# Reading the moving operand backwards in both layers of a convolution and squared-ReLU kernel

## The chip, the cores and the metric

The kernel runs on one core of a Trainium2 chip. The metric is the time of one execution on the device in microseconds; less is better. The profile is one more execution, taken by the hardware profiler, with every instruction's start and duration.

## The reference

The input is x, 8 sequences of 4096 tokens with 192 features. Each feature is convolved over the last 7 tokens of its sequence with softmax weights that belong to its head (8 heads of 24 features). The result goes, token by token, through a two-layer network with 2048 hidden units whose activation is a squared ReLU:

```python
w = np.exp(weight - weight.max(-1, keepdims=True))
w = w / (w.sum(-1, keepdims=True) + 1e-09)
out = np.einsum('hk,bskhg->bshg', w, x_unf)      # x_unf: the last 7 tokens, zeros before the first
x = out.reshape(B * S, D)                        # 32768 x 192
h = x @ w_in                                     # 192 x 2048
r = np.maximum(h, 0.0)
g = s * (r * r) + b
return (g @ w_out).astype(np.float32)            # 2048 x 192
```

The inputs are fp32 except the weights of the network, which come in as float64 words and are converted in the kernel.

## The kernel before

Data lies transposed: features on the 128 partitions, tokens along a partition. The 32768 tokens are 32 super-blocks n of 1024, each two blocks j of 512 tokens. The hidden units are NPAIR = 8 pairs p of two chunks of 128. One step (n, j, p) takes 512 tokens through one pair.

To keep fp32 accuracy at the speed of the type fp32r, which carries fewer mantissa bits, every operand is split into a high and a low part, both fp32r, and a product is three matmuls: weights high by data low, weights high by data high, weights low by data high.

Layer one is the function first. The 192 features are three chunks of 64; the tiles sA, wA, tB and wB hold the convolved tokens, high and low, in such an arrangement that one half of the partitions (rows 0 to 63) works on one chunk of 128 hidden units and the other half (rows 64 to 127) on the other. Each inner call both (line 531) issues two matmuls, one for each half of the rows, with weights of 64 x 128 and a moving operand of 64 x 512. A call of first is 18 matmuls, and fills the PSUM tile h, 128 x 2 x 512: hidden units on partitions, tokens along them, one bank for each chunk.

Between the layers ScalarE takes the ReLU of h into q (line 545) and squares it in place (line 552), VectorE rounds it to the high part qh (line 554) and subtracts to get the low part ql (line 559). All four are elementwise.

Layer two is the function second. Its inner both (line 614) again issues two matmuls, for the two halves of the rows of qh or ql, which are summed into two different PSUM accumulators: w_outB gives the output features 128 to 191 (for the high and the low part of the weights side by side), w_outA the features 0 to 127. A call is 20 matmuls. The accumulators run over all 8 pairs of a block, and are then added, scaled with s and stored. Super-block 0, in which the weights are still being converted, uses second_whole instead, with full-height matmuls of 128 x 128 weights (lines 576, 577, 581 to 583), 10 a step. The very last step of the kernel has its own function last (lines 673, 674 and 686), also with 10 full-height matmuls.

The order of the work on TensorE, VectorE and ScalarE is written out by hand: the calls are traced in the order in which they are to run. Finished steps wait in a Python list, queue, and layer two is issued LAG = 2 steps behind layer one; at the first pair of a block it is held back one step longer, after which two steps of layer two follow each other. While this goes on, VectorE computes the convolution of the super-block to come (lines 161 and 163), and the tiles are swapped and stored by DMAs of the SyncE queue. In the head, before any of this is under way, TensorE computes part of the first convolution in plain fp32 with diagonal matrices as weights (line 257, function conv_tensor): tap k reads 512 columns that begin k columns into xA or xB. The function split_tensor (line 230) and the sums for the bias (function biases) use TensorE as well. None of these three is touched by the change.

Of the kernel before, what the change touches and what calls it, by code (L numbers as in the profile page):

```python
# [17 lines left out]
P = 128  # L18
# [19 lines left out]
def conv_attention_then_squared_relu_mlp(  # L38
# [23 lines left out]
    nc = tc.nc  # L62
# [5 lines left out]
    NF = 2 * NPAIR  # L68
# [206 lines left out]
    def w_in(part, p, chunk, rows):  # L275
        return W[rows, p, part, chunk * P : (chunk + 1) * P]

    def w_outA(part, f, rows=slice(0, P)):
        return W[rows, f // 2, part, CI + f % 2 * P :][:, 0:P]

    def w_outB(f, rows=slice(0, P)):
        return WB[rows, f // 2, f % 2, :]
# [239 lines left out]
    def first(n, j, p, meanwhile=None):  # L522
        h = ps_h.tile([P, 2, BLK], F32, name="h")
        halves = [tok[n].half(j, i) for i in range(2)]

        def both(w, part, at, start, stop):

            for i in range(2):
                chunk = halves[i][at]
                rows = slice(i * HB, (i + 1) * HB)  # L530
                nc.tensor.matmul(  # L531
                    h[:, i, :], w_in(w, p, chunk[0], rows), chunk[part], start=start, stop=stop
                )

        for at in (0, 2, 1):
            both(0, 1, at, at == 0, False)
            both(0, 2, at, False, False)
            both(1, 1, at, False, at == 1)
            if meanwhile and at == 0:
                meanwhile()  # L540
        return h
# [22 lines left out]
    def accumulators(n, j, p):  # L564
        if p == 0:
            acc[n, j] = [ps_o.tile([P, BLK], F32, name=f"acc{k}") for k in (1, 2, 1, 2)[: 4 if n else 2]]
        return acc[n, j]

    def second_whole(n, j, p, qh, ql):


        a1, a2 = accumulators(n, j, p)
        for i in range(2):
            f = 2 * p + i
            st, sp = f == 0, f == NF - 1
            nc.tensor.matmul(a2, w_outB(f), qh[:, i, :], start=st, stop=False)  # L576
            nc.tensor.matmul(a2, w_outB(f), ql[:, i, :], start=False, stop=sp)  # L577
        for i in range(2):
            f = 2 * p + i
            st, sp = f == 0, f == NF - 1  # L580
            nc.tensor.matmul(a1, w_outA(1, f), qh[:, i, :], start=st, stop=False)  # L581
            nc.tensor.matmul(a1, w_outA(0, f), qh[:, i, :], start=False, stop=False)  # L582
            nc.tensor.matmul(a1, w_outA(0, f), ql[:, i, :], start=False, stop=sp)  # L583
        if p == NPAIR - 1:
            t0 = n * SUP + j * BLK
            oA = outs.tile([P, BLK], F32, name="oA")
            nc.scalar.activation(oA, a1, AF.Identity, scale=sb)
            oC = outs.tile([DB, BLK], F32, name="oC", bufs=1)
            nc.scalar.activation(oC, a2[DB:P, :], AF.Identity, scale=sb[DB:P])  # L589
            oB = outs.tile([P, BLK], F32, name="oB")[0:DB]  # L590
            nc.vector.scalar_tensor_tensor(
                oB, a2[0:DB, :], sb[0:DB], oC, op0=ALU.mult, op1=ALU.add
            )
            unbiased.append((oA, outT[0:P, t0 : t0 + BLK], 0))
            unbiased.append((oB, outT[P:D, t0 : t0 + BLK], 2))
            del acc[n, j]
# [7 lines left out]
    def second(n, j, p, qh, ql):  # L604
        if (n, j, p) == steps[-1]:
            return last(n, j, qh, ql)
        accs = accumulators(n, j, p)

        ends = [NF - 1, NF - 1 if (n, j) != steps[-1][:2] else NF - 3]

        def both(to, w, f, q, start=False, stop=False):
            for i in range(2):
                r = slice(i * HB, (i + 1) * HB)
                nc.tensor.matmul(  # L614
                    accs[to + 2 * i], w(f, r), q[r, f % 2, :],
                    start=start and f == 0, stop=stop and f == ends[i],
                )

        for f in (2 * p, 2 * p + 1):
            both(1, w_outB, f, qh, start=True)  # L620
            both(1, w_outB, f, ql, stop=True)
        for f in (2 * p, 2 * p + 1):
            both(0, loA, f, qh, start=True)
            both(0, hiA, f, qh)
            both(0, hiA, f, ql, stop=True)
        if p == NPAIR - 1:
            t0 = n * SUP + j * BLK
            early = (n, j) == (1, 0)

            o = {}  # L630
            for k, name in ((1, "oB"), (0, "oA")):
                o[k] = outs.tile([P, BLK], F32, name=name)
                o[k + 2] = outs.tile([P, BLK], F32, name=name + "2", bufs=1)
                nc.scalar.activation(
                    o[k], accs[k], AF.Identity, scale=sb, bias=0.0 if early else bias[:, k : k + 1]
                )
                nc.scalar.activation(o[k + 2], accs[k + 2], AF.Identity, scale=sb)  # L637
            nc.gpsimd.tensor_tensor(o[1], o[1], o[3], op=ALU.add)  # L638

            oC = outs.tile([DB, BLK], F32, name="oC", bufs=1)  # L640
            nc.sync.dma_start(oC, o[1][DB:P])
            nc.gpsimd.tensor_tensor(o[0], o[0], o[2], op=ALU.add)
            toA, toB = outT[0:P, t0 : t0 + BLK], outT[P:D, t0 : t0 + BLK]
            oB = o[1][0:DB] if early else oC
            if not early:
                nc.sync.dma_start(toA, o[0])
            nc.gpsimd.tensor_tensor(oB, oC, o[1][0:DB], op=ALU.add)
            if early:
                unbiased.extend(((o[0], toA, 0), (oB, toB, 2)))
            else:  # L650
                nc.sync.dma_start(toB, oB)
            del acc[n, j]

    def upper_sums(accs):

        uA = outs.tile([P, BLK], F32, name="oA2", bufs=1)
        uB = outs.tile([DB, BLK], F32, name="oC", bufs=1)
        nc.scalar.activation(
            uB, accs[3][DB:P], AF.Identity, scale=sb[DB:P], bias=bias[DB:P, 1:2]
        )  # L660
        nc.scalar.activation(uA, accs[2], AF.Identity, scale=sb, bias=bias[:, 0:1])
        nc.vector.scalar_tensor_tensor(
            uB, accs[3][0:DB], sb[0:DB], uB, op0=ALU.mult, op1=ALU.add
        )
        return uA, uB

    def last(n, j, qh, ql):

        accs = accumulators(n, j, NPAIR - 1)
        uA, uB = upper_sums(accs)  # L670
        t0 = n * SUP + j * BLK
        for f in (NF - 2, NF - 1):
            nc.tensor.matmul(accs[1], w_outB(f), qh[:, f % 2, :], start=False, stop=False)
            nc.tensor.matmul(accs[1], w_outB(f), ql[:, f % 2, :], start=False, stop=f == NF - 1)
        oB = outs.tile([P, BLK], F32, name="oB")[0:DB]
        nc.vector.scalar_tensor_tensor(
            oB, accs[1][0:DB], sb[0:DB], uB, op0=ALU.mult, op1=ALU.add
        )
        nc.vector.scalar_tensor_tensor(
            oB, accs[1][DB:P], sb[DB:P], oB, op0=ALU.mult, op1=ALU.add  # L680
        )
        nc.sync.dma_start(outT[P:D, t0 : t0 + BLK], oB)
        oA = outs.tile([P, BLK], F32, name="oA")
        for f in (NF - 2, NF - 1):
            for w, q in ((loA, qh), (hiA, qh), (hiA, ql)):
                nc.tensor.matmul(
                    accs[0], w(f, slice(0, P)), q[:, f % 2, :],
                    start=False, stop=f == NF - 1 and q is ql,
                )
        for k, e in enumerate((nc.scalar, nc.sync)):  # L690
            c = slice(k * BLK // 2, (k + 1) * BLK // 2)
            nc.vector.scalar_tensor_tensor(
                oA[:, c], accs[0][:, c], sb, uA[:, c], op0=ALU.mult, op1=ALU.add
            )
            e.dma_start(outT[0:P, t0 + c.start : t0 + c.stop], oA[:, c])
# [65 lines left out]
    with in_order(nc.vector, nc.scalar, nc.tensor):  # L761
        with in_order(nc.sync):
            head()
        headed = last_of(nc.sync)
        for p in range(NPAIR):
            if p > 1:
                if p + 3 < NPAIR:
                    with headed():
                        fetch(p + 3)
                pair(p)  # L770
            if p > 0 and p not in TWICE:
                while len(queue) > (LAG if p < NPAIR - 1 else 0):
                    second_whole(*queue.pop(0))
# [3 lines left out]
    for n, j, p in steps:  # L777
# [7 lines left out]
        with begun() if n == 1 else ExitStack():  # L785
            h = first(n, j, p)
# [62 lines left out]
```

## Time and profile before

| | us |
|---|---|
| median of 3 runs | 2234.78 (2234.44 to 2234.82) |
| span of the profiled execution, first to last instruction | 2232.9 |
| TensorE matmuls busy | 2226.4 |
| TensorE weight loads busy | 1829.1 |
| VectorE busy | 1753.5 |
| ScalarE busy | 1286.4 |
| GpSimd busy | 317.8 |

The span leaves out what lies ahead of the first and behind the last instruction, so it is a little under the time of a run. In the rows, PE is TensorE's matmuls, PEld its weight loads, DVE is VectorE, ACT ScalarE, POOL GpSimd and SP SyncE. A row of groups gives line, engine, operation, output and inputs, their sizes, the count, the busy time in us and the mean duration in ns, and behind the second bar the idle time of the engine just before them with what ended it. Matmuls overlap, so their durations do not add up to time: what counts is the distance from one start to the next. PEclk is the clock that TensorE was granted, in tenths of full speed. A row of the chain or of the timeline begins with the start and the duration in us. A row of waits has the engine and what waited, the releaser, the time in total, the number and the longest.

### The profile page before, as it was taken

The page shows a single profiled execution, that of the slowest core. Times are in us where ns is not written, and L with a number is a line of the kernel's source. Part 1 is how long each engine was busy: PE and PEld are TensorE (multiplying, and loading weights), DVE is VectorE, ACT ScalarE, POOL GpSimd, SP SyncE. Part 2 cuts the span into 40 slices and gives each one's busy share as a digit, 9 for nine tenths or more (in the row PEclk, how much of TensorE's full clock was granted, in tenths as well). Part 3 has the DMA queues.
Part 4 walks back from the last instruction along what each step waited for, and adds up shares of the span by engine and source line. Part 5 has one row for each costly group of instructions (what it writes and reads, how often), then busy time and mean ns, then how long its engine had stood idle before and what let it go on. Part 6 is the DMA issues. An engine that isn't in the chain of part 4 may idle for free.

```text
span 2232.9 us, 45081 instructions
## 1 busy us (share of the span) xinstructions
PE 2226.4 (100%) x19330; PEld 1829.1 (82%) x19330; DVE 1753.5 (79%) x1995; ACT 1286.4 (58%) x1410; POOL 317.8 (14%) x205
## 2 busy tenths in 40 slices
PE   9999999999999999999999999999999999999999
PEld 6788888888888888888888888888888888888887
DVE  8898778777787787777877878778777787787764
ACT  8755555655555555555555555555655555556554
POOL 0022101111011011110110111111101111011110
PEclk9999999999999999999999999999999999999999
DMA  5113112121121111211111111112121121111110
GB/s 180 34 43 87 40 46 62 48 58 44 44 58 53 53 44 45 56 53 53 43 51 50 53 53 53 48 43 62 51 55 44 44 58 53 53 44 42 46 39 17
DMA packets 46168, 117.51 MB, mean 53 GB/s; under 512 B 7760, under 2 KB 8016, under 8 KB 45968
## 3 DMA queue, kind: packets, MB, share of 16 engines
q1 hardware_dynamic: 45824, 114.50, 18.6%
q8 instruction: 151, 2.47, 0.5%
q14 instruction: 49, 0.40, 0.1%
q10 hardware_dynamic: 144, 0.13, 0.0%
HBM read 31.64 MB, written 25.17 MB: 25 GB/s over the span
## 4 chain that ended last, share of the span: by engine, by line
PE 98%; DVE 1%; ACT 1%; DMA 0%; issue 0%; SPq 0%; DVEq 0%
PE acc L614 50%; PE h L531 46%; DVE accA L163 0%; PE acc L576 0%; ACT q L552 0%; DVE ql L559 0%; PE acc L577 0%; PE acc L583 0%; PE acc L582 0%; PE acc L581 0%; ACT qh L554 0%; ACT q L545 0%; DMA xA<-in_xA 0%; DVE t L315 0%; ACT oC L589 0%
## 5 line engine op out<-in xcount | busy, mean ns | idle before, releaser
L545 ACT ACTIVATE q<-h 128x1024 f32<-128x1024 f32 x512 | 525.5, 1026 | 902.8 <-PE h L531 900.4
L559 DVE TENSOR_TENSOR ql<-q,qh 128x1024 fp32r<-128x1024 f32 x512 | 656.7, 1283 | 56.3 <-ACT qh L554 2.6
L554 DVE CAST qh<-q 128x1024 fp32r<-128x1024 f32 x497 | 370.1, 745 | 395.7 <-ACT q L552 393.3
L614 PE MATMUL acc<-qh,W 64*128 64x512 f32 x3960 | 609.9, 386 | 0.0
L552 ACT ACTIVATE q<-q 128x1024 f32<-128x1024 f32 x512 | 543.6, 1062 | 15.9
L614 PEld LDWEIGHTS acc<-qh,W 64*128 64x128 f32 x3960 | 370.9, 184 | 77.9
L531 PE MATMUL h<-sA,W 64*128 64x512 f32 x3072 | 432.4, 387 | 0.0
L531 PE MATMUL h<-wA,W 64*128 64x512 f32 x3072 | 431.6, 386 | 0.0
L531 PE MATMUL h<-tB,W 64*128 64x512 f32 x1536 | 429.9, 386 | 0.0
L531 PE MATMUL h<-wB,W 64*128 64x512 f32 x1536 | 429.9, 386 | 0.0
L614 PE MATMUL acc<-ql,WB 64*128 64x512 f32 x1980 | 385.7, 386 | 0.4 <-DVE ql L559 0.4
L614 PE MATMUL acc<-qh,WB 64*128 64x512 f32 x1980 | 385.6, 386 | 0.0
L614 PE MATMUL acc<-ql,W 64*128 64x512 f32 x1980 | 385.5, 386 | 0.0
L638 POOL TENSOR_TENSOR oB<-oB,oB 128x512 f32<-128x512 f32 x61 | 115.2, 1889 | 1672.7 <-ACT oB L637 1672.7
L163 DVE SCALAR_TENSOR_TENSOR accA<-xA,tap,accA 128x512 f32<-128x512 f32 x378 | 341.5, 903 | 6.8
L531 PEld LDWEIGHTS h<-sA,W 64*128 64x128 f32 x3072 | 287.3, 184 | 62.9 <-issue 1.1
L531 PEld LDWEIGHTS h<-wA,W 64*128 64x128 f32 x3072 | 287.8, 184 | 60.4
L531 PEld LDWEIGHTS h<-tB,W 64*128 64x128 f32 x1536 | 282.6, 184 | 40.5 <-issue 0.2
L531 PEld LDWEIGHTS h<-wB,W 64*128 64x128 f32 x1536 | 282.5, 184 | 20.1
L614 PEld LDWEIGHTS acc<-ql,WB 64*128 64x128 f32 x1980 | 185.5, 184 | 40.1 <-DVE ql L559 1.3
L614 PEld LDWEIGHTS acc<-ql,W 64*128 64x128 f32 x1980 | 185.5, 184 | 39.0
L614 PEld LDWEIGHTS acc<-qh,WB 64*128 64x128 f32 x1980 | 185.5, 184 | 38.8
(115 smaller groups left out, 1035.4 us busy)
## 6 DMA issues: line engine op xcount, KB each, us to landing
wA<-sA SPq DMA_DIRECT2D x126, 256.0 KB, 3.6
outT<-oA SPq DMA_DIRECT2D x63, 256.0 KB, 2.0
wB<-tB SPq DMA_DIRECT2D x60, 256.0 KB, 3.4
xA<-in_xA SPq DMA_DIRECT2D x24, 515.0 KB, 3.6
xB<-in_xB SPq DMA_DIRECT2D x32, 259.0 KB, 2.6
oC<-oB SPq DMA_DIRECT2D x61, 128.0 KB, 2.2
outT<-oC SPq DMA_DIRECT2D x60, 128.0 KB, 2.3
words<-in_w SPq DMA_DIRECT2D x7, 768.0 KB, 6.2
```

The source lines that it names most:

```text
L163: nc.vector.scalar_tensor_tensor(acc, src, w[:, k : k + 1], acc, op0=ALU.mult, op1=ALU.add)
L531: nc.tensor.matmul(h[:, i, :], w_in(w, p, chunk[0], rows), chunk[part], start=start, stop=stop)
L545: nc.scalar.activation(q, h, AF.Relu)
L552: nc.scalar.activation(q, q, AF.Square)
L554: cast(qh, q)
L559: nc.vector.tensor_tensor(ql, q, qh.bitcast(F32), op=ALU.subtract)
L614: nc.tensor.matmul(accs[to + 2 * i], w(f, r), q[r, f % 2, :], start=start and f == 0, stop=stop and f == ends[i],)
L638: nc.gpsimd.tensor_tensor(o[1], o[1], o[3], op=ALU.add)
```

## The change

Every matmul of the two layers reads its moving operand from the last column to the first: the slice of 512 columns gets a step of minus one. The operand's tile, size and type, the weights and the output are as before. Layer one so writes the tokens of a block into h in reverse, the elementwise steps keep them in that order in q, qh and ql, and layer two, which reads qh and ql from the last column to the first, writes them into its accumulators in their own order. The matmuls of the head's convolution, of split_tensor and of the bias read upwards as before. The instructions of each engine, their order and their waits are the same in both programs.

```diff
@@ first @@
-                    h[:, i, :], w_in(w, p, chunk[0], rows), chunk[part], start=start, stop=stop
+                    h[:, i, :], w_in(w, p, chunk[0], rows), chunk[part][:, ::-1], start=start, stop=stop
@@ second_whole @@
-            nc.tensor.matmul(a2, w_outB(f), qh[:, i, :], start=st, stop=False)
-            nc.tensor.matmul(a2, w_outB(f), ql[:, i, :], start=False, stop=sp)
+            nc.tensor.matmul(a2, w_outB(f), qh[:, i, ::-1], start=st, stop=False)
+            nc.tensor.matmul(a2, w_outB(f), ql[:, i, ::-1], start=False, stop=sp)
...
-            nc.tensor.matmul(a1, w_outA(1, f), qh[:, i, :], start=st, stop=False)
-            nc.tensor.matmul(a1, w_outA(0, f), qh[:, i, :], start=False, stop=False)
-            nc.tensor.matmul(a1, w_outA(0, f), ql[:, i, :], start=False, stop=sp)
+            nc.tensor.matmul(a1, w_outA(1, f), qh[:, i, ::-1], start=st, stop=False)
+            nc.tensor.matmul(a1, w_outA(0, f), qh[:, i, ::-1], start=False, stop=False)
+            nc.tensor.matmul(a1, w_outA(0, f), ql[:, i, ::-1], start=False, stop=sp)
@@ second @@
-                    accs[to + 2 * i], w(f, r), q[r, f % 2, :],
+                    accs[to + 2 * i], w(f, r), q[r, f % 2, ::-1],
@@ last @@
-            nc.tensor.matmul(accs[1], w_outB(f), qh[:, f % 2, :], start=False, stop=False)
-            nc.tensor.matmul(accs[1], w_outB(f), ql[:, f % 2, :], start=False, stop=f == NF - 1)
+            nc.tensor.matmul(accs[1], w_outB(f), qh[:, f % 2, ::-1], start=False, stop=False)
+            nc.tensor.matmul(accs[1], w_outB(f), ql[:, f % 2, ::-1], start=False, stop=f == NF - 1)
...
-                    accs[0], w(f, slice(0, P)), q[:, f % 2, :],
+                    accs[0], w(f, slice(0, P)), q[:, f % 2, ::-1],
```

## The prediction

> **What bounds the kernel now.** I read the page's first parts before anything else, since they say whether there is any engine whose work decides the end.
>
> ```profile
> PE 2226.4 (100%) x19330; PEld 1829.1 (82%) x19330; DVE 1753.5 (79%) x1995; ACT 1286.4 (58%) x1410; POOL 317.8 (14%) x205
> PEclk9999999999999999999999999999999999999999
> PE 98%; DVE 1%; ACT 1%; DMA 0%; issue 0%; SPq 0%; DVEq 0%
> PE acc L614 50%; PE h L531 46%; DVE accA L163 0%; PE acc L576 0%; ACT q L552 0%; DVE ql L559 0%; PE acc L577 0%; PE acc L583 0%; PE acc L582 0%; PE acc L581 0%; ACT qh L554 0%; ACT q L545 0%; DMA xA<-in_xA 0%; DVE t L315 0%; ACT oC L589 0%
> ```
>
> TensorE is busy for the whole span, its granted clock never falls, and the chain of work that ended last is 98% TensorE: 50% of it is layer two (line 614), 46% layer one (line 531). A busy TensorE can still be one that waits inside the pipeline, so I next read what it waited for, in the list of waits for that engine alone.
>
> ```profile
> PE acc L388 <- POOL xA L145: 1.0, 1, 1.0
> PE acc L230 <- ACT sA L227: 0.4, 1, 0.4
> PE acc L614 <- DVE ql L559: 0.4, 1, 0.4
> PE acc L230 <- ACT hiB L227: 0.2, 1, 0.2
> ```
>
> That is the whole list: 2.0 us in four waits, three of them in the head. After the head, one wait of 0.4 us is on record. So nothing that another engine does sets the pace; the pace is the rate at which TensorE takes matmuls. The chain in order of time gives this rate. It has one piece of 40 layer-two matmuls in each block of 512 tokens (two of the drained steps back to back), and I quote the first and the last of a run of such pieces that are all the same distance apart.
>
> ```profile
> 203.55 4.53 PE acc L614 x40
> 1822.85 4.53 PE acc L614 x40
> ```
>
> Between these two starts lie 1619.30 us, and 47 blocks at 34.453 us each. A block is 8 steps p, and a step is 18 matmuls of layer one and 20 of layer two. These are issued in twos, one on rows 0 to 63 and one on rows 64 to 127 of the array, which run side by side; I call such a pair a slot. 19 slots a step and 8 steps a block make 152 slots, so a slot takes 34.453 / 152 = 226.66 ns. The timeline of one step in the middle shows the same thing in single instructions.
>
> ```profile
> 1000.34 0.84 PE L531 MATMUL h<-sA,W 64*128 64x512 f32 x6
> 1001.02 0.39 PE L531 MATMUL h<-tB,W 64*128 64x512 f32 x1
> 1001.70 0.84 PE L531 MATMUL h<-wA,W 64*128 64x512 f32 x6
> ```
>
> From the sA reads to the first tB read there are 3 slots in 0.68 us, and again 3 from there to the wA reads: 227 ns each, within the rounding of the rows. A single matmul is shown as 386 ns long, but since it overlaps its neighbours, the distance from start to start is what counts. That the distance holds to a hundredth over 47 blocks, whatever VectorE, ScalarE and the DMAs do beside it, tells me that it belongs to the instruction itself.
>
> The number of slots comes from the groups of instructions by line.
>
> ```profile
> L614 PE MATMUL acc<-qh,W 64*128 64x512 f32 x3960 | 609.9, 386 | 0.0
> L531 PE MATMUL h<-sA,W 64*128 64x512 f32 x3072 | 432.4, 387 | 0.0
> L531 PE MATMUL h<-wA,W 64*128 64x512 f32 x3072 | 431.6, 386 | 0.0
> L531 PE MATMUL h<-tB,W 64*128 64x512 f32 x1536 | 429.9, 386 | 0.0
> L531 PE MATMUL h<-wB,W 64*128 64x512 f32 x1536 | 429.9, 386 | 0.0
> L614 PE MATMUL acc<-ql,WB 64*128 64x512 f32 x1980 | 385.7, 386 | 0.4 <-DVE ql L559 0.4
> L614 PE MATMUL acc<-qh,WB 64*128 64x512 f32 x1980 | 385.6, 386 | 0.0
> L614 PE MATMUL acc<-ql,W 64*128 64x512 f32 x1980 | 385.5, 386 | 0.0
> L576 PE MATMUL acc<-qh,WB 128*128 128x512 f32 x32 | 13.0, 407 | 0.0
> ```
>
> Layer one has 3072 + 3072 + 1536 + 1536 = 9216 matmuls of 64 rows, 4608 slots. Layer two has 3960 + 3 x 1980 = 9900, 4950 slots. The first two blocks use full-height matmuls instead, five groups of 32 like the last row, 160 slots of one matmul each, and the function last has 10 more. Together 9728 slots, and 9728 x 226.66 ns = 2204.9 us of the 2232.9 us span. The 28.0 us that are left are the head up to the first layer-one matmul, its gaps, and the tail. The runs' median of 2234.78 us is 1.9 us above the span; I carry these 1.9 us through unchanged.
>
> **The change part by part.** All of it is one thing: the start and the sign of the step of the moving operand in the matmuls of lines 531, 576, 577, 581 to 583, 614, 673, 674 and 686. The operand's pattern starts at its last column and steps by minus one; its size, its type, its partitions, the weights and the PSUM output, which is written from first to last column as before, stay. Layer one therefore leaves h in reversed token order, the squaring on ScalarE and VectorE is elementwise and carries the order along, and layer two reverses it back into acc, so that what is stored is in order.
>
> Instructions: none is added or removed on any engine, and the order and the waits of each engine's list are those of before. So there is no queue that a step is moved past, no DMA more or less, and no new wait: 0 us, with one answer. The data that each matmul needs are the same tiles, and each tile is waited for as a whole before its first column is read, so that reading the last column first starts nothing earlier or later: 0 us. ScalarE, VectorE and GpSimd read and write the same addresses in the same direction: 0 us.
>
> What is left is the price of a descending read in TensorE, once for each of the 9728 slots. Of it the trace of before has no instance: every operand in it ascends, so this price has to be bounded by rows. The nearest rows on where a read begins are those of the convolution in the head, which TensorE does in plain fp32 at line 257. Tap k reads 512 columns that begin k columns into the tile, so its reads begin at every place in a short stretch of memory, and each tap is two records on the timeline.
>
> ```profile
> 7.57 3.17 PE L257 MATMUL acc<-xB,q 128*128 128x512 f32 x7
> 10.57 1.88 PE L257 MATMUL acc<-xA,q 128*128 128x512 f32 x4
> 12.96 4.46 PE L257 MATMUL acc<-xA,q 128*128 128x512 f32 x10
> 17.34 0.98 PE L531 MATMUL h<-sA,W 64*128 64x512 f32 x6
> ```
>
> The first stretch is 7 records (the later taps, xB) in 10.57 - 7.57 = 3.00 us up to the next start, 428.6 ns each. The second is 4 records (taps 0 and 1): less the last record's own 592 ns, (1.88 - 0.59) / 3 = 430 ns. The third is 10 records (taps 2 to 6): (4.46 - 0.59) / 9 = 430 ns. They agree within 1.4 ns although they begin at different offsets. So a start at another column than the tile's first costs between nothing and 1.4 ns here, at a rate that is about half that of the kernel's main matmuls. Per slot that is 0 to 1.4 ns, over 9728 slots 0 to 13.6 us. I take 0, because most of these 1.4 ns is the rounding of the rows.
>
> For the rate of the descending read itself the far bound is the same rows read another way: the slowest steady pass over 512 columns that TensorE shows with its clock fully granted takes 428.6 ns against 226.66 ns. If a descending fp32r read fell to that rate, a slot would cost 201.9 ns more and the kernel 9728 x 0.2019 = 1964 us more. The other end is below nothing: the same pass halved, as if fp32r streamed exactly twice as fast as a plain pass, is 214.3 ns, so that 12.4 ns of each slot are not explained by the streaming of columns; if the direction removed all of them, the kernel would lose 9728 x 0.0124 = 120.6 us. Between these ends I take 0: with the step's size unchanged, a descending read touches the same words in the same number of steps, and the nearest row for it is the ascending read at 226.66 ns.
>
> To these 12.4 ns a rule of the Trainium skill can be held. Its page "TensorE: Matmul & The Clock Gate", section "Back-to-back issue gap", gives N / 2.4 + 2.5 ns from one warm matmul to the next, 215.8 ns for 512 columns, which would make 9728 slots an estimated 2099 us; the trace disagrees with 226.66 ns and 2205 us, and the measurement decides. The page does not say what fills the difference.
>
> Another page of the Trainium skill, "Advanced Engine Details and Errata", section "SBUF Cachelines", says that reads run at full rate as long as successive ones fall into the same line of 16 bytes, two in a line at the least. By that rule a step of minus one fp32 word, with four reads in each line, would leave the sum as it is; no run here shows it so far.
>
> The sum: 2232.9 + 0 = 2232.9 us of span, and with the 1.9 us around it 2234.8 us.
>
> **The rivals.** The first is slower by little: a price at each start. The place is the beginning of each matmul's read, at the end of a tile instead of its first column. Since TensorE has no idle time to hide it, it adds up 9728 times. It decides from 0.2% on, that is 4.47 us, or 0.46 ns per slot. At the 1.4 ns of the tap rows it makes 2234.8 + 13.6 = 2248.4 us. For it speaks that nothing covers even half a nanosecond; against it that taps with seven different starts show no pitch that grows.
>
> The second is slower by much: the descending read is not streamed at full rate. The same instructions, but every column pays. At the pitch of the plain fp32 passes the result is 2234.8 + 1964 = 4199 us, and anything between is possible. For it speaks that no descending operand exists in this trace and that no other matmul in it takes columns as fast as these, so that a fetch which joins neighbouring words only upwards would be felt at once. Against it: the slot's 226.66 ns is the same for 64 and 128 rows and over all sources, so the read shows no sign of being near a limit that varies. VectorE could not become late in its place: a slower TensorE gives the others more time.
>
> The third is faster: the unexplained 12.4 ns go. If they were a cost at the turn from one matmul's last address back to the next one's first, the direction could matter. All of it gone would give 2234.8 - 120.6 = 2114 us. TensorE would still be the bound, since VectorE has room:
>
> ```profile
> 600.00:1000.00 400.00, 400.00 (x3532) 330.58 (x3532) 314.23 (x347) 227.11 (x245) 59.79 (x38) 1.00 0.19 51
> ```
>
> In 400 us of the middle, VectorE is busy for 314.23 us (third figure) and ScalarE for 227.11 us, and a gain of 12.4 ns in 226.66 would shorten these 400 us to 378. Against this rival speaks that a matmul which turns from one operand to the next jumps in either direction, and both directions jump equally far.
>
> **How the numbers follow.** The forecast, no price, gets 0.77. The small price at a start gets 0.09, the rate that falls 0.09, the gain 0.05. That the edit changes nothing on the chip because the pattern would be undone on the way is within the first case, as its time is the same. A measurement of this kernel can tell 0.2%, about 4.5 us, from no change; so within 0.2% is 0.77, slower 0.18, faster 0.05. The predicted time is 2234.8 us. The range begins 0.2% below it, at 2230.3, and reaches up to the small price's 2248.4; it holds 0.77 + 0.09 and leaves out 0.14, the large loss and the gain.
>
> **What would show it.** If the forecast is right, the same pieces of 40 matmuls in the chain stand 34.45 us apart, a matmul of lines 531 and 614 is 386 ns long, and the list of TensorE's waits stays at four short ones. A price at the start would show as blocks of up to 152 x 1.4 = 213 ns more, with matmuls that are hardly longer. A read that falls in rate would show in the duration of each matmul and in a block of up to 65 us, with VectorE's and ScalarE's idle time growing by as much and their own durations as before. A gain would show as blocks down to 32.6 us. If the span moved while a block stayed at 34.45 us, the head or the tail would be the place, and my reasoning about the waits would be wrong.

## The result and the profile after

The changed kernel takes 2297.49 us (median of 4 runs, 2297.40 to 2297.74) against 2234.80 us of the kernel before on the same chip (4 runs): a ratio of 1.0281, with a 95% interval of 1.0268 to 1.0293. It is 62.7 us slower. The forecast was no change, and the time lies outside the range given.

The first parts of the page after show which engine has the loss.

```profile
PE 2290.3 (100%) x19330; PEld 1839.0 (80%) x19330; DVE 1752.8 (76%) x1995; ACT 1287.3 (56%) x1410; POOL 316.8 (14%) x205
PEclk9999999999999999999999999999999999999999
PE 100%; DVE 0%; DVEq 0%; issue 0%; POOL 0%; POOLq 0%
L614 PE MATMUL acc<-qh,W 64*128 64x512 f32 x3960 | 624.4, 394 | 0.0
L531 PE MATMUL h<-sA,W 64*128 64x512 f32 x3072 | 443.0, 394 | 0.0
L559 DVE TENSOR_TENSOR ql<-q,qh 128x1024 fp32r<-128x1024 f32 x512 | 658.2, 1285 | 56.9 <-ACT qh L554 3.3
```

The counts are those of before, the granted clock is full, and VectorE's and ScalarE's operations are as long as they were (ql: 1285 ns against 1283). Only TensorE's matmuls have grown, from 386 to 394 ns, in both layers alike. The list of what TensorE waited for has become shorter, one row of 1.0 us in the head. So no wait has come in. The chain in order of time has its pieces of 40 layer-two matmuls again:

```profile
206.94 4.67 PE acc L614 x40
...
1164.53 4.67 PE acc L614 x40
```

Between these two lie 27 blocks, 957.59 / 27 = 35.466 us each; before it was 34.453. With 152 slots in a block (a slot is a pair of matmuls on the two halves of the rows, started side by side), a slot now takes 233.33 ns, 6.67 ns more than the 226.66 of before. In the timeline of the changed kernel every three slots lie 0.70 us apart, where there were 0.68:

```profile
1000.57 0.86 PE L531 MATMUL h<-sA,W 64*128 64x512 f32 x6
1001.27 0.39 PE L531 MATMUL h<-tB,W 64*128 64x512 f32 x1
1001.97 0.86 PE L531 MATMUL h<-wA,W 64*128 64x512 f32 x6
```

9728 slots x 6.67 ns = 64.9 us, and the span has grown by 2295.8 - 2232.9 = 62.9 us. The 2 us between belong to the first 121 us. The 25th step of layer one starts at 121.3 us before and at 122.3 us after, only 1.0 us later; from there on each slot pays in full. Up to there, 1.0 us of TensorE's waits has gone from the list, and in super-block 0 not every slot of before was as short as 226.7 ns: its full-height matmuls started 228.4 ns apart in the mean (149 distances, six gaps of more than 300 ns left out), where they now start 233.4 apart. Behind the head the loss is thus one steady price at each slot. What is left to find is what the price is for.

### The profile page after: what moved, and what is told of

It reads as the page before. It is cut to its first block, busy times and chain, and to the rows that moved or that the text cites. A ratio compares the mean times of both kernels' runs of the same rounds, so it can differ in the third digit from the quotient of the medians.

```text
span 2295.8 us, 45081 instructions
## 1 busy us (share of the span) xinstructions
PE 2290.3 (100%) x19330; PEld 1839.0 (80%) x19330; DVE 1752.8 (76%) x1995; ACT 1287.3 (56%) x1410; POOL 316.8 (14%) x205
## 4 chain that ended last, share of the span: by engine, by line
PE 100%; DVE 0%; DVEq 0%; issue 0%; POOL 0%; POOLq 0%
PE acc L614 50%; PE h L531 47%; PE acc L257 1%; PE acc L576 0%; PE acc L583 0%; PE acc L577 0%; PE acc L582 0%; PE acc L581 0%; PE acc L388 0%; DVE oB L676 0%; PE acc L673 0%; PE acc L230 0%; DVE oB L679 0%; DVEq L845 0%; PE acc L674 0%
## 5 line engine op out<-in xcount | busy, mean ns | idle before, releaser
L559 DVE TENSOR_TENSOR ql<-q,qh 128x1024 fp32r<-128x1024 f32 x512 | 658.2, 1285 | 56.9 <-ACT qh L554 3.3
L614 PE MATMUL acc<-qh,W 64*128 64x512 f32 x3960 | 624.4, 394 | 0.0
L531 PE MATMUL h<-sA,W 64*128 64x512 f32 x3072 | 443.0, 394 | 0.0
L531 PE MATMUL h<-wA,W 64*128 64x512 f32 x3072 | 442.4, 394 | 0.0
L531 PE MATMUL h<-tB,W 64*128 64x512 f32 x1536 | 440.8, 394 | 0.0
L531 PE MATMUL h<-wB,W 64*128 64x512 f32 x1536 | 440.8, 394 | 0.0
L614 PE MATMUL acc<-ql,WB 64*128 64x512 f32 x1980 | 393.5, 394 | 0.0
L614 PE MATMUL acc<-qh,WB 64*128 64x512 f32 x1980 | 393.4, 394 | 0.0
L614 PE MATMUL acc<-ql,W 64*128 64x512 f32 x1980 | 393.4, 394 | 0.0
```

The source lines that it names most:

```text
L531: nc.tensor.matmul(h[:, i, :], w_in(w, p, chunk[0], rows), chunk[part][:, ::-1], start=start, stop=stop)
L559: nc.vector.tensor_tensor(ql, q, qh.bitcast(F32), op=ALU.subtract)
L614: nc.tensor.matmul(accs[to + 2 * i], w(f, r), q[r, f % 2, ::-1], start=start and f == 0, stop=stop and f == ends[i],)
```

## The experiments

Numbers of slots below are distances between the starts of successive matmuls of one half of the rows, read from the trace in ns and averaged over some 55 steps each. Where a kernel gives each of the eight steps p its own form of layer one, one profile tells eight forms apart; in these, layer two reads upwards as before, and the first slots after a change of form are a transition. A few kernels have a line or more ahead of the matmul, which moves line numbers.

### One layer alone, and four questions on the read

Layer one only: the diff of the change in the function first alone.

> Only layer one reads backwards; layer two reads upwards, so that each block's tokens come out reversed. The changed kernel has 152 slots in a block of 35.466 us, 233.33 ns a slot, 6.67 ns more than before. Theory A, a price at every descending matmul wherever it stands: 4608 slots x 6.67 ns = 30.7 us more than before, 2265.5 us, and layer-two slots stay at 226.7 ns. Rival, a price of the turn from one layer's direction to the other's buffers or of the memory that layer two reads: all of the 62.7 us or none of it, 2297 or 2235 us.

Measured: 2272.95 us against 2234.66 (ratio 1.0172, interval 1.0155 to 1.0189), 38.3 us more, neither 30.7 nor 62.7. The timeline at the change from downward layer one to upward layer two shows what the expectation left out.

```profile
1000.31 0.86 PE L531 MATMUL h<-wA,W 64*128 64x512 f32 x6
1001.01 0.40 PE L614 MATMUL acc<-qh,WB 64*128 64x512 f32 x2
1001.25 0.40 PE L614 MATMUL acc<-ql,WB 64*128 64x512 f32 x2
1001.48 0.39 PE L614 MATMUL acc<-qh,WB 64*128 64x512 f32 x2
1001.71 0.39 PE L614 MATMUL acc<-ql,WB 64*128 64x512 f32 x2
1001.93 0.62 PE L614 MATMUL acc<-qh,W 64*128 64x512 f32 x4
```

The first two upward slots take 238.3 and 231.7 ns in the averages (0.24 and 0.23 us in the rows), and then 226.7 each; the first three downward slots of a step take 232.5, 240.0 and 230.8 before they settle at 233.3. A change down and up again costs 16.7 + 3.3 = 20 ns. There are 7 such in a block of 8 steps, since two steps of the same layer follow each other once, and 62 blocks: 8.7 us. The slots of layer two, settled, are at their old value. So each descending slot pays, and a turn costs extra for two or three slots.

Sizes and steps:

```diff
+                cols, step = (512, 1) if start else ((512, 1), (512, -1), (384, 1), (384, -1), (256, 1), (256, -1), (256, 2), (256, -2))[p]
+                x = chunk[part][:, 0 : cols * abs(step)][:, ::step]
```

> Layer two as before. In layer one the first of the nine slots of a step is an upward read of 512 columns, the other eight read, for p = 0 to 7: 512 up, 512 down, 384 up, 384 down, 256 up, 256 down, every second column of 512 up (256 columns), the same down; the columns left out are left out of the sums. Theory A, a fixed price at each descending matmul: down is 6.7 ns above up at all three sizes. Theory B, a price for each column read downwards: 6.7 ns at 512, 5.0 at 384, 3.3 at 256. By either, a step of two columns up costs about what 256 columns up cost; a rival of both, that any step other than plus one costs, has plus two slower than plus one too.

| columns, step | up | down | difference |
|---|---|---|---|
| 512, one | 226.7 | 233.3 | +6.7 |
| 384, one | 173.3 | 177.8 | +4.4 |
| 256, one | 120.0 | 118.3 | -1.7 |
| 256, two | 226.6 to 236.7 | 233.3 | |

(ns a slot, settled.) Both theories miss: the difference is neither fixed nor in proportion, and at 256 columns the descending read is the faster one. And a step of two costs as much as twice the columns, whatever its sign. The timeline rows of 256 columns with step one (upward) and with step two (upward) show it without any averaging:

```profile
1012.23 0.28 PE L533 MATMUL h<-tB,W 64*128 64x256 f32 x1
1012.59 0.52 PE L533 MATMUL h<-wA,W 64*128 64x256 f32 x6
...
1019.35 0.41 PE L533 MATMUL h<-tB,W 64*128 64x256 f32 x1
1020.05 0.87 PE L533 MATMUL h<-wA,W 64*128 64x256 f32 x6
```

Three slots of 256 neighbouring columns take 0.36 us; three slots of 256 columns with gaps take 0.70. So with a step of two the slot's time goes with the memory that is gone through and not with the columns. This suggests, and does not yet show for a step of one, that the read has nothing in hand: what the read loses, the slot loses.

Starts, upward and downward, with 384 columns (the downward kernel has [:, ::-1] behind the slice):

```diff
+                at0 = (0, 1, 2, 4, 8, 16, 32, 64)[p]
+                x = chunk[part] if start else chunk[part][:, at0 : at0 + 384]
```

> All reads upwards. In layer one the first slot of a step reads 512 columns, the other eight 384 columns that begin at column 0, 1, 2, 4, 8, 16, 32, 64 of the tile for p = 0 to 7; 128 columns are left out of the sums. Theories A and B, that the direction is what costs: all eight slots alike. Theory C, that a read which begins inside an aligned piece of memory costs 6.7 ns whatever its direction (a descending read begins at a tile's last word): a slot is 6.7 ns longer at column 1 and 2, and on up to the column at which the piece is a whole one again.

> Like the upward run with 384 columns from column 0, 1, 2, 4, 8, 16, 32, 64, but read from the last of these columns to the first. Theory C, a price of beginning inside an aligned piece: column 1 makes the read begin at column 384, the first word of a line, and would be the cheapest. Theory D: starts 0 and 64 alike, the others different in their single slots, all of them around 173 to 180 ns.

| first column | 0 | 1 | 2 | 4 | 8 | 16 | 32 | 64 |
|---|---|---|---|---|---|---|---|---|
| up, ns | 173.3 | 178.3 | 173.3 | 175.6 | 176.7 | 173.3 | 175.6 | 173.3 |
| down, ns | 177.8 | 177.8 | 177.8 | 180.0 | 175.6 | 176.7 | 176.7 | 177.8 |

Theory C, that a read pays for beginning inside an aligned piece, does not survive: the values go up and down with the start. But direction alone does not either, as upward reads vary by 5 ns. One thing is exact: the slots of start 64 are those of start 0, one after the other to a nanosecond, transition included, in both directions (up: 171, 175, 177.5, 185, 176, 182, 173.3). What counts repeats every 64 columns, 256 bytes.

Orders within the read:

```diff
+                lines = x.rearrange("p (a b) -> p a b", b=4)
+                blocks = x.rearrange("p (a b) -> p a b", b=128)
+                x = (
+                    lambda: lines, lambda: lines[:, ::-1, ::-1], lambda: lines[:, ::-1, :],
+                    lambda: lines[:, :, ::-1], lambda: blocks[:, ::-1, :], lambda: blocks[:, :, ::-1],
+                    lambda: x[:, ::-1] if i else x, lambda: x[:, ::-1] if (w, part) == (0, 2) else x,
+                )[p]()
```

> Layer two as before. In layer one the 512 columns are read, for p = 0 to 7: upwards; downwards; lines of four words downwards with the words of a line upwards; lines upwards with their words downwards; blocks of 128 columns downwards, words upwards; blocks upwards, words downwards; rows 64 to 127 downwards and rows 0 to 63 upwards; only the matmuls with low data downwards, one slot of three. Sums are permuted by it. Theory B1, the order of the words in a line costs: p = 1, 3, 5 at 233.3 ns, p = 2 and 4 at 226.7. Theory B2, the order of the lines costs: p = 1 and 2 at 233.3, p = 3 at 226.7, p = 4 close to 226.7. Theories A and C, a price where a read begins: p = 1 at 233.3, p = 3 and 5 too by theory C since they begin inside a line, p = 2 and 4 by theory A only if the sign of the address's course counts. By all of them p = 6 is at 233.3 for a pair runs at the pace of its slower half, and p = 7 has 6.7 ns more in every third slot; a price of turning round would have more there.

| p | order | ns a slot, settled |
|---|---|---|
| 0 | upwards | 226.7 |
| 1 | downwards | 233.3 |
| 2 | lines of 4 words down, words up | 233.3 |
| 3 | lines up, words down | 226.7 |
| 4 | blocks of 128 down, words up | 226.7 |
| 5 | blocks up, words down | 233.3 |

Theory B2 holds: the order in which lines of 16 bytes are visited pays, and the order of the words within a line does not. (That the piece is 16 bytes and not a larger one, these orders do not tell.) That blocks of 128 columns may be visited downwards for nothing fits the period of 64: modulo 256 bytes, such a read is an upward one. With p = 7, each descending slot among upward ones costs 6.7 ns, spread over two slots (232.5, 227.5). With p = 6 the expectation failed: only the half of the rows that reads downwards pays, and the other one goes on at 226.7. The two halves are not held together slot by slot; the lag between them goes from 0.24 to 0.72 us and no further, so over a whole block both lose alike:

```profile
1008.32 0.39 PE L542 MATMUL h<-sA,W 64*128 64x512 f32 x1
1008.52 0.39 PE L623 MATMUL acc<-qh,W 64*128 64x512 f32 x1
1008.55 0.39 PE L542 MATMUL h<-sA,W 64*128 64x512 f32 x1
1008.74 0.39 PE L623 MATMUL acc<-ql,W 64*128 64x512 f32 x1
```

One half is in layer one while the other still works on layer two.

### The weights

What else reads these partitions? Under each slot TensorE loads the weights of the next, as the trace of before shows for the matmul of tB that starts at 1001.02 us:

```profile
1000.80 0.18 PEld L531 LDWEIGHTS h<-tB,W 64*128 64x128 f32 x1
```

I turned to these.

```diff
+                wide, apart, down = (
+                    (128, 1, 0), (128, 1, 1), (64, 1, 0), (64, 1, 1),
+                    (32, 1, 0), (32, 1, 1), (128, 2, 0), (128, 4, 0),
+                )[p] if not (start or stop) else (128, 1, 0)
+                c0 = chunk[0] * P if apart == 1 else chunk[0] * HB
+                w_ = W[rows, p, w, c0 : c0 + wide * apart : apart]
```

> Theory D, formed after the first four runs: a slot is 512 columns of streaming, about 213.3 ns, and what the moving read loses to the weight load of the next slot, which reads 128 columns of other memory on the same partitions in the same time; upwards it loses 13.3 ns, downwards 20. In layer one, outside the first and last slot of a step, the weights are, for p = 0 to 7: 128 columns with an upward and with a downward moving read, 64 columns with each, 32 columns with each, every second column of 256 (upward read), every fourth column of 512 (upward read). With fewer columns a part of the hidden units is left out of the sums, with the last two other weights are used. Theory D: 226.7 and 233.3 ns; with 64 columns 220.0 and 223.3; with 32 columns 216.7 and 218.3; with weights spread over twice and four times the memory more than 226.7. Theories A and B, a price of the moving read alone: 226.7 and 233.3 whatever the weights.

```diff
+                wide, down = (
+                    (96, 0), (96, 1), (16, 0), (16, 1), (4, 0), (4, 1), (1, 0), (1, 1)
+                )[p] if not (start or stop) else (128, 0)
```

> With 64 and 32 weight columns an upward slot took about 231 and 232 ns instead of 226.7, a downward one stayed near 233: the loss does not shrink with the weights, so that theory D in the form of a price for each line of the weights has fallen. Here layer one has, outside the first and the last slot of a step, 96, 16, 4 and 1 columns of weights, each with an upward and a downward moving read (the other hidden units are left out of these sums). Theory E, that a slot loses about 20 ns by itself and the upward read with 128 columns of weights meets a phase in which it loses only 13.3: 233 ns for all with few columns, up and down alike at 1 column. Theory F, that the loss comes from the two reads meeting and the count of meetings is what the phase decides: with 1 column next to nothing is left to meet and both directions fall to about 213 to 216 ns.

| weight columns | 128 | 96 | 64 | 32 | 16 | 4 | 1 |
|---|---|---|---|---|---|---|---|
| up, ns | 226.7 | 230 | 231 | 232 | 231.1 | 231.1 | 231.1 |
| down, ns | 233.3 | 233.3 | 233.3 | 233.3 | 233.3 | 233.3 | 233.3 |

(Upward ones with fewer columns do not settle at one value but go round in a few: 225.8, 234.2, 233.3 with 16, 4 and 1 column.) Theory D, a price for each line of the weights, falls, and so does theory F: with one column of weights the load takes 79 ns in the trace, against 184 with 128, and the upward slot is longer, not shorter. Theory E comes nearest: an upward read loses about as much as a downward one, except with the full 128 columns. The rows with one column, of an upward and then of a downward step:

```profile
1021.07 0.39 PE L535 MATMUL h<-tB,W 64*1 64x512 f32 x1
1021.76 0.85 PE L535 MATMUL h<-wA,W 64*1 64x512 f32 x6
...
1025.42 0.39 PE L535 MATMUL h<-tB,W 64*1 64x512 f32 x1
1026.12 0.87 PE L535 MATMUL h<-wA,W 64*1 64x512 f32 x6
```

Three slots take 0.69 us upwards and 0.70 downwards: nearly the whole difference between the directions is gone, and it is gone by the upward one's loss. Weights spread over twice and four times the memory gave 233.3 and 235.0 ns with an upward read.

So the question is no longer why the downward read is slow, but why the upward one was fast. The next kernels moved the two reads against each other: the weights' first column by a few columns, and the moving operand's first column by the same.

```diff
+                off, down = ((0, 0), (8, 0), (16, 0), (32, 0), (0, 1), (8, 1), (16, 1), (32, 1))[p]
+                c0 = chunk[0] * P + off
+                x = chunk[part][:, ::-1] if down else chunk[part]
...
+                    h[:, i, :], W[rows, p, w, c0 : c0 + P], x, start=start, stop=stop
```

> The weights of layer one begin 0, 8, 16, 32 columns further on than before (so that other weights are used), with the moving operand read upwards for p = 0 to 3 and downwards for p = 4 to 7. Theory D with a pattern of memory that repeats every 64 columns: the pitch is moved by the first slots after a change of phase and then returns to 226.7 up and 233.3 down, since each lost turn moves the phase on; or it stays at another value for some starts, in which case there is a start that is faster than 226.7. Theory A: 226.7 and 233.3 at all starts from the first slot on.

> Weights of layer one begin 0, 4, 24, 40, 48, 56 columns further on with an upward read, 24 and 48 with a downward one (so that other weights are used). In the first such run 0 columns gave 226.7 ns, 8 and 16 gave 233.3 on average, 32 columns a mixture around 232; downwards 0, 8 and 16 gave 233.3, 32 gave 236.7. If the weights' place is one half of the cause: values between 226 and 240 that differ by start, in steps of one eighth of 6.67 ns, and 56 and 48 need not be like 8 and 16. If the weights' place had nothing to do with it, and the first run's differences came from other causes: 226.7 for all upward ones.

```diff
+            flat = lambda t: t[r].rearrange("p a b -> p (a b)")
...
+                at0 = (0, 8, 16, 24, 32, 40, 48, 56)[p]
+                x = chunk[3][:, at0 : at0 + BLK]
```

> Weights as before; the upward moving read of 512 columns of layer one begins 0, 8, 16, 24, 32, 40, 48, 56 columns into a tile whose high and low parts lie behind each other (so that high and low parts are mixed in the sums). If only the distance between the two reads counts, modulo 64 columns, a moving read that begins k further on equals weights that begin 64 - k further on: 32 as weights 32 (about 232 ns), 48 as weights 16 and 56 as weights 8 (233.3 on average). If the moving read's own place counts: another order, and weights' starts and moving starts are not related.

| weights on by | 0 | 4 | 8 | 16 | 24 | 40 | 48 | 56 |
|---|---|---|---|---|---|---|---|---|
| up, ns | 226.7 | 226.7 | 233.3 | 233.3 | 233.9 | 233.3 | 228.9 | 233.3 |
| down, ns | 233.3 | | 233.3 | 233.3 | 233.3 | | 233.3 | |

(24: mean of the last eight slots of the step, which had not settled. 32: upward still in transition at the end of the step, 228 to 241; downward 235.0 and 238.3 in turn.) For k = 8, 24, 48 and 56, the moving operand moved by 64 - k gives the same as the weights moved by k, down to the single slots: weights 8 on, 235.0 and 231.7 in turn; moving operand 56 on, 235.0 and 231.7. Weights 24 on: 231.7, 237.5, 237.5, 230.8, 234.2, 235.0; moving 40 on: 231.6, 237.5, 237.5, 230.8, 234.2, 235.0. Weights 48 on: 229.2, 231.7, 225.8; moving 16 on the same three. At the other three distances the single slots differ: at 16 both average 233.3, but the weights moved give 230.8 and 235.8 in turn and the moving operand moved a flat 233.3; at 32 (moving operand: 229.2 and 237.5 in turn) and 40 the two kernels were not in the same round. So with 128 columns of weights the distance of the two reads modulo 64 columns decides whether a slot is short, and the slots ahead have a part in which round it falls into. All tiles that the two layers of the kernel before read begin at the same place modulo 256 bytes, going by their sizes, which are whole multiples of 64 columns (the trace shows no addresses): distance 0, which is the favourable one.

### The whole kernel, with the weights moved

If that is so, the loss must come without any backward reading. For 64 bytes of distance between the operands one line is enough:

```diff
+    ctx.enter_context(tc.tile_pool(name="pad", bufs=1)).tile([P, 16], F32, name="pad")
     wide_w = ctx.enter_context(tc.tile_pool(name="wide_w", bufs=1))
```

> The kernel before with all reads upwards, but 16 unused columns (64 bytes) ahead of the two weight tiles, so that weights and moving operands no longer begin at the same place modulo 64 columns. Theory G, that the two reads' distance modulo 64 columns decides: layer one's slots with weights 16 columns on alternated between 235.8 and 230.8 ns, 233.3 on average, so the whole kernel takes 9728 x 6.67 = 65 us more, about 2299 us, like the changed kernel though nothing is read backwards. Theory A, a price of the descending read: 2234.7 us.

Its counterpart moves all operands together:

```diff
-GAP = 296
+GAP = 296 + 16
```

> The kernel before with 16 more unused columns ahead of all moving operands and all weights, so that everything moves by 64 bytes together. Theory G, the distance decides: 2234.7 us, slots of 226.7 ns. If the places count each by itself, as the alignment of a read to some piece of memory: slots of 228 to 233 ns and 2250 to 2299 us.

> The changed kernel, all reads of the two layers downwards, with the weight tiles 16 columns on. Layer one's downward slots were 233.3 ns with weights 0 and 16 columns on alike, so by theory G as measured so far nothing changes: 2297.5 us. If a downward read has its favourable place a quarter of 64 columns away, 2235 us.

| kernel | us | ratio to before | interval |
|---|---|---|---|
| changed: read downwards | 2297.49 | 1.0281 | 1.0268 to 1.0293 |
| weights_moved: upwards, weights 16 columns on | 2297.62 | 1.0282 | 1.0266 to 1.0297 |
| all_moved: upwards, all 16 columns on | 2234.91 | 1.0001 | 0.9991 to 1.0010 |
| weights_moved_down: downwards, weights 16 on | 2297.95 | 1.0283 | 1.0266 to 1.0300 |

Sixteen unused columns cost what the change costs, and nothing in the arithmetic, the order or the direction differs from the kernel before. (The tiles allocated behind the weights move with them; neither layer reads those, and TensorE's list of waits is one row of 1.0 us in weights_moved as in the changed kernel.) Both causes together cost no more than either alone, 63.3 us and not twice as much, so they are not two prices that add up. The chain of weights_moved and then that of all_moved show the same blocks as the changed kernel and as the kernel before:

```profile
207.26 4.67 PE acc L615 x40
...
1200.33 4.67 PE acc L615 x40
```

```profile
203.90 4.53 PE acc L614 x40
...
1754.30 4.53 PE acc L614 x40
```

Weights_moved has 28 blocks in 993.07 us, 35.467 each; all_moved 45 blocks in 1550.40 us, 34.453 each. In weights_moved the slots alternate between 230.8 and 235.8 ns, in both layers, as they had in the probe of layer one.

One more kernel looked for other places, with weight_starts' code and other numbers, and the last whole-layer kernel has layer two alone backwards.

> Weights of layer one 0, 2, 12, 62 columns on with an upward read and 4, 40, 56, 60 columns on with a downward one. So far upward: 0 and 4 at 226.7, 48 at 228.9, 8, 16, 24, 40, 56 at 233 to 234 ns; downward: 0, 8, 16, 24, 48 at 233.3, 32 at 236.7. If the direction had no price of its own and only met a worse place, one of the downward starts left should come near 226.7. If no start does, the descending read has a price beside the place. For upward reads, a place better than 226.7 ns would show here if it lies close to 0; I expect 2 and 62 at 226.7, 12 between 227 and 234.

Upward: 226.7 at 0, a round of 229.2 to 234.2 at 2, 233.3 at 12 and at 62. Downward: 233.3 at 4, 40, 56 and 60. So the good place is narrow: 2 columns to either side of it are bad again, where I had expected 226.7. Of the ten places tried in all none brings the downward read below 233.3. By the words of the expectation the descending read thus has a price beside the place. But weights_moved_down shows that it does not come on top of that of a bad place.

> Only layer two reads backwards, so that each block's tokens come out reversed. Layer one only was 38.3 us above before: 4608 slots x 6.67 ns = 30.7 us, and 20 ns at each change from an upward to a downward step and back, some 430 times. Theory D, that a change of direction moves the phase of the two reads and costs a few slots until it settles: here 4950 x 6.67 = 33.0 us and again 7.6 us, 2275.3 us. A price by matmul alone: 33.0 us, 2267.7 us. A price of the memory of sA, wA, tB and wB: 2235 us and little more.

Measured: 2276.28 us against 2234.62 (ratio 1.0187, interval 1.0170 to 1.0204), 41.7 us more: 33.0 for 4950 slots and 8.7 for the turns (20 ns x 434). With turns counted by blocks the sum is right to 0.1 us, and layer one's 30.7 + 8.7 = 39.4 is 1.1 us above its measured 38.3, which I put down to the head. The agreement for layer two is in part luck: this kernel also reads its 170 full-height matmuls downwards, which at the same price would add 1.1 us, and the head, where 160 of them lie, takes in about as much.

## Why the prediction was wrong

**What bounds the kernel** was right, and so was the count of 9728 slots: they carry the loss, 6.67 ns each behind the head. Instructions, waits and the other engines cost nothing, as forecast.

**The step that failed** is the sentence in which I took 0 between the two ends: that with the step's size unchanged a descending read touches the same words in the same number of steps, so that the ascending 226.66 ns is its nearest row. This takes the slot's time for a property of the moving read alone. The runs showed that it is one of two reads together: the upward read gets 226.7 ns only where 128 columns of weights are loaded beneath it that lie at the same place modulo 64 columns (or 4 on), and 229 to 234 ns at the other places tried. The descending read visits the lines in the other order and takes 233.3 at nine of ten places of the weights, 236.7 at the tenth. That it loses the same relation to the weights is the likely reading and not shown, as no place was found at which it is fast.

**The argument against the large rival** failed with it. I read from the equal 226.66 ns of all sources that the read was not near a limit. The sources were alike because all their tiles begin at the same place modulo 256 bytes, so the trace of before held the condition constant that it would have had to vary. The time was not quite constant even there: of the 149 distances between full-height matmuls in super-block 0, 45 are 228 to 236 ns, all of them upward reads. The step of two shows how near the limit the read is: 256 columns spread over 512 take the time of 512. The sign that I had given for this rival came, in longer matmuls (394 ns for 386) and a block of 35.47 us, but the loss was neither a fixed price nor in proportion to the columns.

**The bounds.** The 0 to 1.4 ns from the taps of the convolution missed 6.67 by far, and the other end, 201.9 ns, was no help. The taps run at about half the rate; such a stream can lose turns without its time showing it, which is argued from the rates and was not tried. The 12.4 ns that I could not explain in each slot turned out to be the term in question: I asked whether they could vanish, and not whether they could grow.

**The pages.** The rule on lines of 16 bytes in "SBUF Cachelines" of the Trainium skill's "Advanced Engine Details and Errata" asks for at least two reads in a line. Two are not enough here: a step of two words has two in each line and takes 0.70 us for three slots against 0.36. The 215.8 ns of "Back-to-back issue gap" in the Trainium skill's "TensorE: Matmul & The Clock Gate" is given there for isolated matmuls; of a stream of weight loads and matmuls the section says that both set the spacing, which I passed over in the prediction. No settled slot of 512 columns came down to 215.8 ns on average; the lowest were at 226.7.

**What stays open.** How the two reads get into each other's way is not shown: which of them is held up, and why the load of 128 columns at distance 0 costs a slot less than that of one column (226.7 against 231.1). Why the descending read is slow at every place is open too. Descending weights were not tried. The period of 256 bytes, the order of lines as the thing that counts and, for upward reads, the distance as the deciding quantity are shown; a picture of banks behind it would be a guess. That all upward kernels with a bad distance come so close to 233.3, the downward value, is measured and not explained.

## What to carry to other kernels

If a profile's bound is a stream of equal instructions, its time per instruction is not a constant of the engine: before taking it for one, ask what it shares its memory with and whether the trace ever varied that. For kernels that are bound by such matmuls, lay moving operands and weights at the same place modulo 256 bytes (here all_moved shows that they may move together freely), and read the moving operand upwards; 64 bytes between them cost 2.8%. This is shown for fp32r, 512 columns and 128 columns of weights alone. To price an access pattern that the trace does not hold, one kernel with another pattern in each step of a loop gives eight answers in one profile.

## What the runs showed of the hardware

- The loss of a slot comes in steps of 0.83 ns and depends on the slots ahead: after a change of direction it needs two or three slots, after others six or more, and then stays at one value or goes round in a few.
- The two halves of the rows run as separate streams within limits. Where one lost 6.7 ns a slot, it fell behind the other by 656 ns in the median and by 718 at most, and the later matmuls of the one half began before earlier ones of the other.
- With steps of one and two columns, the time of an fp32r matmul goes with the memory that its moving operand spans, not with its columns: 256 neighbouring columns take 120.0 ns a slot, every second one of 512 about 230.
